# q of the first two units in packets of two positions, decay factors on GpSimd's queue, fillers behind the first scores

## The chip, the cores and the metric

The kernel runs on one core of a Trainium2 chip. The metric is the device time of one execution in microseconds. Profiles are of one execution; times inside them count from the start of its span.

## The reference

A retention block is followed by a multiplicative feed-forward block, both in float32 or wider:

```python
# q, k, v: (8 batches, 8 heads, 576 positions, 64)
scores = q @ k.T / sqrt(64)
Dmat   = where(i >= j, gamma[h] ** (i - j), 0)      # gamma[h] = 1 - 2**(-5-h)
ret    = (scores * Dmat) @ v
x      = ret.transpose(0, 2, 1, 3).reshape(4608, 512)
out    = ((x @ w1) * (x @ w2)) @ w3 @ w_out         # w1, w2: 512x1024, w3: 1024x1024, w_out: 1024x512
```

The four weights come in as 64-bit floats and are converted on the chip.

## The kernel before

The retention is computed in 20 units. A unit is a pair of batches and a chunk of positions; the chunks of a pair have 64, 128, 128, 128 and 128 positions. Units 0 to 4 are the first pair. Units are numbered g, with chunk c = g % 5.

The decay matrix is split into a factor for q, gamma^i / 8, and one for k, gamma^-j. They come as two small inputs, decay_q (8 heads x 576) and decay_k (576 x 8 heads). decay_q is fetched into dq as it lies, turned by five small TensorE transposes into the PSUM tile gps (L122) and copied by VectorE to gq (L125), where positions lie on partitions. decay_k is fetched straight into gk, by two transfers on ScalarE's DMA queue (L115, L116).

For each unit `load` (L87) fetches k, q and v: positions on partitions, and 2 batches x 8 heads x 64 values in each. A run that is contiguous in memory is one position of one head, 64 values, 256 bytes. Then

- `scale` (L195) multiplies q by gq (VectorE at L204 for units 0 and 1, ScalarE later) and v by gk (GpSimd at L204 for units 0 and 1);
- `front` (L207) transposes k and q by TensorE, two heads at a time, into a PSUM tile tp, and ScalarE copies it to kT and qT (L221), which have a head's values on partitions and positions along the row;
- `score` (L224) multiplies kT by qT into four PSUM tiles sc (L233); VectorE multiplies them by the causal mask into pm (L236);
- `state` (L240) adds k^T v to a state st (L255), which ScalarE copies to sb (L259);
- `pv_state` and `pv` multiply the state and pm into the output tiles xps (L274, L299), and ScalarE evicts them to xT (L306), the tokens of the second block.

The feed-forward block runs on blocks of tokens of 192 positions with one or two levels of Strassen's scheme; its VectorE sums (L149, L496, L533) and products (`up`, L528) begin at about 28 us and take the rest of the time. The weights are fetched in blocks by `load_block` on SP's queue (L342, L345), and converted by ScalarE (L395 to L397) and VectorE (L399, L402, L413, L426). `convert(n)` does n steps of that conversion.

All order is written out by hand: every engine takes its instructions in the order of the program text. The text at the start issues, on SP's queue, k and q of unit 0, weight block 0, v of unit 0, block 1, k and q of unit 1, block 2, v of unit 1, block 3, and then the loads of units 2, 3 and 4 with further blocks. ScalarE's queue issues dq and the two parts of gk. GpSimd makes the identity and the mask. TensorE runs ten products of the identity with itself (`idle`), and `keep_busy(n)` (L127) puts n more of them at other places; they write a PSUM tile that nobody reads. A float32 product shows as two passes in the profile.

The lines of the start that the change touches (L733 to L755):

```python
    scale(0, "q", engine=nc.vector)
    front(0, "k")
    keep_busy(4)
    front(0, "q")
    convert(2)
    score(0)
    scale(0, "v")
    state(0)
    convert_up_to(1)
    pv(0)()
    ...
    front(1, "k")
    keep_busy(4)
    scale(1, "q", engine=nc.vector)
    front(1, "q")
```

SBUF tiles come from pools, in which a tag has a fixed number of buffers that are taken in turn: "ld_q" has two, "T" five, "ab" two, "c" one. The PSUM pool "acc" has seven.

Of the kernel before, what the change touches and what calls it, by code (L numbers as in the profile page):

```python
# [8 lines left out]
F32 = mybir.dt.float32  # L9
# [4 lines left out]
ALU = mybir.AluOpType  # L14
# [5 lines left out]
def kernel(  # L20
# [13 lines left out]
    nc = tc.nc  # L34
    moe_w1, moe_w2, moe_w3, moe_w_out = (
        w.bitcast(I32).rearrange("r (c t) -> r c t", t=2) for w in (moe_w1, moe_w2, moe_w3, moe_w_out))
    B, H, S, D = q.shape
# [3 lines left out]
    P = 128  # L41
# [6 lines left out]
    NC = (S + P - 1) // P  # L48
    short = S - (NC - 1) * P
    sizes = [short] + [P] * (NC - 1)  # L50
    starts = [0] + [short + c * P for c in range(NC - 1)]
    G = NB2 * NC
    NB = 3
    TB = S // NB
    NT = 2 * TB // P
    KD = DM // P
    KF = DF // P
# [4 lines left out]
    const = ctx.enter_context(tc.tile_pool(name="const", bufs=1))  # L62
    wp = ctx.enter_context(tc.tile_pool(name="wp", bufs=1))
    ffn = ctx.enter_context(tc.tile_pool(name="ffn", bufs=2))
# [6 lines left out]
    pools = {}  # L71
# [9 lines left out]
    acc = acc_part.enter_context(tc.tile_pool(name="acc", bufs=7, space=PSUM))  # L81
# [3 lines left out]
    live = {}  # L85

    def load(g, names, engine=nc.sync):  # L87
        i, c = divmod(g, NC)
        sz = sizes[c]
        src = {"k": k, "q": q, "v": v}  # L90
        for nm in names:
            t = pools["ld"].tile([P, 2 * H, D], F32, tag="ld_" + nm, name="ld_" + nm)
            engine.dma_start(
                t[:sz], src[nm][2 * i:2 * i + 2, :, starts[c]:starts[c] + sz, :].rearrange("b h p d -> p (b h) d"))
            live[nm, g] = t

    dq = ffn.tile([P, 4, 2, TB], F32, tag="c", name="dq", bufs=1).rearrange("p a b s -> p (a b s)")[:H, :S]
    nc.scalar.dma_start(dq, decay_q)
    load(0, "k")
    load(0, "q")  # L100

    ident = const.tile([P, P], F32, tag="ident", name="ident")
    make_identity(nc, ident)
# [8 lines left out]
    gk = const.tile([P, NC, H], F32, tag="gk", name="gk")  # L112
    gq = const.tile([P, NC, H], F32, tag="gq", name="gq")
    gqs = const.tile([P, NP, S // 32], F32, tag="gqs", name="gqs")
    nc.scalar.dma_start(gk[:short, 0, :], decay_k[:short, :])  # L115
    nc.scalar.dma_start(gk[:, 1:, :], decay_k[short:, :].rearrange("(c p) h -> p c h", p=P))  # L116
    warm = acc.tile([P, P], F32, tag="acc", name="idle")
    for _ in range(10):
        nc.tensor.matmul(warm, ident, ident, start=True, stop=True)
    gps = acc.tile([P, NC, H], F32, tag="acc", name="gps")  # L120
    for c in range(NC):
        nc.tensor.transpose(gps[:sizes[c], c, :], dq[:, starts[c]:starts[c] + sizes[c]], ident[:H, :H])  # L122
    for c in (0, slice(1, NC)):
        n = short if c == 0 else P
        nc.vector.tensor_copy(gq[:n, c, :], gps[:n, c, :])  # L125

    def keep_busy(n):  # L127

        t = acc.tile([P, P], F32, tag="acc", name="idle")
        for _ in range(n):  # L130
            nc.tensor.matmul(t, ident, ident, start=True, stop=True)
# [63 lines left out]
    def scale(g, nm, scalar=False, engine=nc.gpsimd):  # L195
        c = g % NC
        sz = sizes[c]
        t, gam = live[nm, g], {"q": gq, "v": gk}[nm]
        t = t[:sz].rearrange("p (b h) d -> p b h d", b=2)
        if scalar:  # L200
            for h in range(H) if scalar is True else scalar:
                nc.scalar.mul(t[:, :, h, :], t[:, :, h, :], gam[:sz, c, h:h + 1])
            return
        engine.tensor_tensor(  # L204
            out=t, in0=t, in1=gam[:sz, c].unsqueeze(1).unsqueeze(3).to_broadcast([sz, 2, H, D]), op=ALU.mult)

    def front(g, names="kq"):  # L207
        c = g % NC
        sz = sizes[c]
        for nm in names:  # L210
            src = live[nm, g]
            dst = pools["fr"].tile([P, 2, NP, P], F32, tag=nm + "T", name=nm + "T",
                                   bufs=1 if nm == "k" and g >= NC else 2)
            for b in range(2):
                tp = acc.tile([P, NP, P], F32, tag="acc", name="tp")
                for p in range(NP):
                    h = b * H + 2 * p
                    nc.tensor.transpose(tp[:, p, :sz],  # L218
                                        src[:sz, h:h + 2, :].rearrange("p a d -> p (a d)"),
                                        ident[:sz, :sz])  # L220
                nc.scalar.copy(dst[:, b, :, :sz], tp[:, :, :sz])  # L221
            live[nm + "T", g] = dst

    def score(g):  # L224
        c = g % NC
        sz = sizes[c]
        kT, qT = live["kT", g], live["qT", g]
        pm = pools["fr"].tile([P, 2, 2, NP, P], F32, tag="pm", name="pm", bufs=1)
        for b in range(2):
            sc = [acc.tile([P, NP, P], F32, tag="acc", name="sc") for j in range(2)]  # L230
            for p in range(NP):
                for j, hs in enumerate(heads):
                    nc.tensor.matmul(sc[j][:sz, p, :sz], kT[hs, b, p, :sz], qT[hs, b, p, :sz],  # L233
                                     start=True, stop=True)
            for j in range(2):
                nc.vector.tensor_mul(pm[:sz, b, j, :, :sz], sc[j][:sz, :, :sz],  # L236
                                     mask[:sz, :sz].unsqueeze(1).to_broadcast([sz, NP, sz]))
        live["pm", g] = pm

    def state(g):  # L240
        c = g % NC
        sz = sizes[c]
        if c == NC - 1:
            return
        vs = live["v", g]
        kn = live["k", g]
        if c == 0:
            live["st"] = st_ps.tile([P, 2, NP, D], F32, tag="st", name="st")
        st = live["st"]

        for b in range(2):
            for p in range(NP):
                for j, hs in enumerate(heads):
                    h = b * H + 2 * p + j
                    nc.tensor.matmul(st[hs, b, p, :], kn[:sz, h, :], vs[:sz, h, :],  # L255
                                     start=(c == 0 and b == 0 and p == 0), stop=(c == NC - 2),
                                     skip_group_check=True)
        sb = pools["fr"].tile([P, 2, NP, D], F32, tag="sb", name="sb")
        nc.scalar.copy(sb, st)  # L259
        live["sb", g + 1] = sb  # L260
# [64 lines left out]
    def load_block():  # L325
        n = loaded[0]
        if n == len(blocks):
            return
        key, w = blocks[n]
        t = raw.tile([P, CV, 2], I32, tag="raw", name="raw", bufs=5)  # L330
        if key[0] in ("A", "w12"):
            if key[0] == "A":
                _, r, f = key
                t4 = t.rearrange("p (j c n) t -> p j c n t", j=2, c=2)
                parts = [(t4[:, j], w[:, f * P:(f + 1) * P]) for j, w in enumerate((moe_w1, moe_w2))]
            else:
                _, fp, _, r = key
                parts = [(t.rearrange("p (c n) t -> p c n t", c=2), w[:, fp * QC:(fp + 1) * QC])]
            for t2, src in parts:
                src = src[2 * r * P:2 * (r + 1) * P]  # L340
                if r == 0:
                    nc.sync.dma_start(t2, src.rearrange("(c p) n t -> p c n t", p=P))  # L342
                else:
                    for half in range(2):
                        nc.sync.dma_start(t2[heads[half]],  # L345
                                          src.rearrange("(c a d) n t -> a d c n t", a=2, d=D)[1 - half])
        elif key[0] == "wo":
            src = w.rearrange("(a i x) n t -> i a x n t", i=KF, x=BL)[key[1]]
            for a in range(QP):
                nc.sync.dma_start(t[a * BL:(a + 1) * BL], src[a])  # L350
        else:
            _, ft, h = key
            src = w[ft * P:(ft + 1) * P].rearrange("(j r) (a h f) t -> h a r j f t", r=BL, a=QP, h=DF // CV)
            for a in range(QP):
                nc.sync.dma_start(t[a * BL:(a + 1) * BL].rearrange("p (j f) t -> p j f t", j=P // BL), src[h, a])
        live["raw", n] = t
        loaded[0] += 1
# [105 lines left out]
    def convert(n):  # L463

        for _ in range(n):
            if go_on() is not None:
                return
# [105 lines left out]
    g = 0  # L573
# [152 lines left out]
    load_block()  # L726
    load(0, "v")
    load_block()
    load(1, "kq")
    load_block()  # L730
    load(1, "v")
    load_block()
# [1 line left out]
    front(0, "k")  # L734
    keep_busy(4)
    front(0, "q")
    convert(2)
    score(0)
    scale(0, "v")
    state(0)  # L740
    convert_up_to(1)
# [403 lines left out]
    g = NC  # L1145
# [9 lines left out]
    for g in first_pair:  # L1155
        n = (1, 1, 2, 2)[g - NC]
# [38 lines left out]
    g = 2 * NC - 1  # L1195
# [10 lines left out]
    g = 2 * NC  # L1206
# [14 lines left out]
    for g in range(2 * NC, G):  # L1221
        n = dealt[g - 2 * NC]
# [42 lines left out]
    g = G  # L1265
# [44 lines left out]
```

## Time and profile before

| | us |
|---|---|
| three runs | 835.0, 838.52, 838.6 |
| median of the three | 838.52 |
| the profiled execution | 836.28 |
| its span | 834.6 |
| TensorE busy in the span | 816.1 (98%) |
| VectorE busy | 545.4 (65%) |
| ScalarE busy | 291.7 (35%) |
| GpSimd busy | 216.2 (26%) |

The span runs from the first instruction to the last; what the profiled execution took beyond it, 1.7 us, lies around it. Busy shares are means over stages that have different limits. The page cuts the span in 40 slices of 20.9 us and gives a digit of tenths for each engine. A busy TensorE need not be at its peak, since the ends of matmuls are modelled.

### The profile page before, as it was taken

The numbers are of one execution on the slowest core, as the hardware profiler recorded it, in microseconds if no ns is written. First come the engines' busy times: TensorE is split into PE (matmuls) and PEld (weight loads), VectorE is DVE, ScalarE is ACT, GpSimd is POOL, SyncE is SP. The second block draws the span as 40 slices with busy tenths as digits, with TensorE's granted clock in tenths as the row PEclk, the third lists the DMA queues.
The fourth block names the chain that finished last, engine by engine and source line by source line (L and its number), as shares of the span: only waits on it lengthen the run. The fifth ranks groups of instructions, "written<-read, shape, count | busy, mean of one in ns | idle before, by whom it ended". The sixth has DMA issues, their size and how long they took to land.

```text
span 834.6 us, 15774 instructions
## 1 busy us (share of the span) xinstructions
PE 816.1 (98%) x6095; PEld 735.5 (88%) x6095; DVE 545.4 (65%) x962; ACT 291.7 (35%) x609; POOL 216.2 (26%) x247
## 2 busy tenths in 40 slices
PE   7999999999999999989999999999999999999998
PEld 7889999744888998779999889998889998899987
DVE  4899999992554558754657755577745667646653
ACT  4787556581111011245453024342034331033300
POOL 1000000001102353005556105555006461045600
PEclk8999999999999999999999999999999999999999
DMA  9995464446035668997876537978245453046311
GB/s 195 222 220 138 78 142 132 114 119 109 6 76 120 101 162 285 278 291 193 211 226 178 109 80 206 223 238 221 57 96 177 159 195 114 34 149 215 139 30 47
DMA packets 197484, 126.96 MB, mean 152 GB/s; under 512 B 157848, under 2 KB 179096, under 8 KB 197408
## 3 DMA queue, kind: packets, MB, share of 16 engines
q1 hardware_dynamic: 168560, 50.40, 29.5%
q0 software_dynamic: 11824, 63.31, 23.0%
q10 hardware_dynamic: 17024, 12.23, 5.3%
q8 instruction: 48, 0.79, 0.4%
q14 instruction: 28, 0.23, 0.1%
HBM read 103.62 MB, written 22.28 MB: 151 GB/s over the span
## 4 chain that ended last, share of the span: by engine, by line
PE 83%; DVE 7%; DMA 6%; issue 2%; SPq 1%; ACT 0%; POOL 0%; ACTq 0%; DVEq 0%
PE po L645 21%; PE up L1052 17%; PE up L528 14%; PE seed L1052 13%; PE ps L477 7%; PE xps L299 3%; PE sc L233 3%; PE xps L274 1%; DMA ld_v<-in_v_dram 1%; SPq L171 1%; PE tp L218 1%; DMA out_dram<-ot 1%; DMA ld_q<-in_q_dram 1%; PE st L255 1%; DVE ab L1024 1%
## 5 line engine op out<-in xcount | busy, mean ns | idle before, releaser
L645 PE MATMUL po<-w3o,ab 128*128 128x256 f32 x552 | 125.1, 381 | 4.0 <-DVE ot L649 3.2
L645 PEld LDWEIGHTS po<-w3o,ab 128*128 128x128 f32 x552 | 103.7, 190 | 20.8 <-DVE ot L649 5.1
L1057 POOL TENSOR_TENSOR cc<-cc 128x384 f32<-128x384 f32 x112 | 109.3, 1002 | 3.8 <-ACT cc L1075 2.4
L1064 DVE TENSOR_TENSOR cc<-seed,cc 128x384 f32<-128x384 f32 x88 | 48.6, 552 | 69.1 <-PE seed L1052 60.1
L181 POOL TENSOR_TENSOR bl_q<-bl_q,gqs 128x512 f32<-128x512 f32 (+1 forms) x26 | 25.9, 1014 | 187.8 <-DMA bl_q<-in_q_dram 184.4
L1052 PE MATMUL up<-xT,ra 128*128 128x192 f32 x384 | 73.5, 328 | 0.0
L528 PE MATMUL up<-xT,wA 128*128 128x192 f32 x384 | 70.7, 328 | 0.8 <-DVE xT L496 0.8
L533 DVE TENSOR_TENSOR c<-up,c 128x384 f32<-128x384 f32 x80 | 44.0, 550 | 39.6 <-PE up L528 39.2
L236 DVE TENSOR_TENSOR pm<-sc,mask 128x512 f32<-128x512 f32 (+1 forms) x80 | 45.3, 627 | 34.9 <-PE sc L233 34.8
L1064 DVE TENSOR_TENSOR cc<-up,cc 128x384 f32<-128x384 f32 x88 | 48.4, 550 | 29.8 <-PE up L1052 21.8
L528 PEld LDWEIGHTS up<-xT,wA 128*128 128x128 f32 x384 | 63.3, 190 | 2.2 <-PE up L528 1.1
L645 PE MATMUL po<-wB,forms 128*128 128x256 f32 x288 | 65.1, 379 | 0.0
L1052 PEld LDWEIGHTS up<-xT,ra 128*128 128x128 f32 x384 | 63.8, 190 | 1.0
L645 PEld LDWEIGHTS po<-wB,forms 128*128 128x128 f32 x288 | 54.7, 190 | 7.4
L1071 ACT COPY seed<-up 128x384 f32<-128x384 f32 x56 | 25.9, 463 | 100.2 <-PE up L1052 55.2
L953 POOL DMA_DIRECT2D ra<-kept x53 | 30.0, 565 | 117.7 <-PE seed L1052 88.5
L477 PE MATMUL ps<-wo,w3T 128*128 128x512 f32 x128 | 55.1, 592 | 0.0
L1052 PE MATMUL up<-ra 128*128 128x192 f32 x288 | 54.7, 326 | 0.0
L1052 PE MATMUL seed<-e,ra 128*128 128x192 f32 x256 | 50.9, 329 | 0.0
L477 PEld LDWEIGHTS ps<-wo,w3T 128*128 128x128 f32 x128 | 24.3, 190 | 30.1 <-issue 29.7
L1052 PEld LDWEIGHTS up<-ra 128*128 128x128 f32 x288 | 48.1, 190 | 0.1
L528 PE MATMUL up<-T,wS 128*128 128x192 f32 x256 | 46.7, 326 | 1.4 <-DVE wS L149 1.4
(129 smaller groups left out, 1467.5 us busy)
## 6 DMA issues: line engine op xcount, KB each, us to landing
ra<-kept POOLq DMA_DIRECT2D x53, 896.0 KB, 5.0
raw<-in_moe_w_dram SPq DMA_DIRECT2D x72, 128.0 KB, 3.0
out_dram<-ot ACTq DMA_DIRECT2D x50, 128.0 KB, 2.3
bl_q<-in_q_dram SPq DMA_DIRECT2D x192, 32.0 KB, 3.1
bl_k<-in_k_dram SPq DMA_DIRECT2D x136, 32.0 KB, 3.3
raw<-in_moe_w_dram SPq DMA_DIRECT2D x16, 256.0 KB, 6.4
ld_k<-in_k_dram SPq DMA_DIRECT2D x8, 512.0 KB, 6.2
raw<-in_moe_w_out_dram SPq DMA_DIRECT2D x32, 128.0 KB, 2.7
```

The source lines that it names most:

```text
L181: nc.gpsimd.tensor_tensor(out=part, in0=part, in1=gqs[:, :, n0:n0 + n].unsqueeze(3).to_broadcast([P, NP, n, BL]), op=ALU.mult)
L233: nc.tensor.matmul(sc[j][:sz, p, :sz], kT[hs, b, p, :sz], qT[hs, b, p, :sz], start=True, stop=True)
L236: nc.vector.tensor_mul(pm[:sz, b, j, :, :sz], sc[j][:sz, :, :sz], mask[:sz, :sz].unsqueeze(1).to_broadcast([sz, NP, sz]))
L477: nc.tensor.matmul(ps, live["w3T", ft][:, g, :], live["wo"][:, g, :], start=(g == 0), stop=(g == KF - 1))
L528: nc.tensor.matmul(ps[:, w, :], a[:, w, r, :], b[:, r, :], start=(new and w == r == 0), stop=(w == r == 1), skip_group_check=True)
L533: nc.vector.tensor_add(c[:, to], ps, c[:, sb])
L645: nc.tensor.matmul(ps[nm], a[A][:, f, :], live["W"][B][:, f, :], start=(f == 0 and not on), stop=(f == NP - 1), skip_group_check=True)
L953: engine.dma_start(ring[n % 3], kept[n % 14 // 7][nm])
L1052: nc.tensor.matmul(ps[:, w, :], weight_of(slot, a, w), B[b], start=(new and w == 0), stop=True, skip_group_check=True)
L1057: nc.gpsimd.tensor_tensor(out=o, in0=o, in1=i, op=ALU.add)
L1064: nc.vector.tensor_add(c[:, j], ps, with_add[:, j])
L1071: nc.scalar.copy(p6, p1)
```

## The change

- **q of units 0 and 1** is fetched by a new `load_pairs`. A partition now holds two neighbouring positions of one batch; the two batches lie on two halves of the partitions, and each is a transfer of its own. A contiguous run is two positions of a head, 512 bytes.
- **Their scaling** (`scale` for q of g < 2) is two instructions instead of one, one for each position of the pair (j), each for eight heads. They write a new tile q2, which takes one buffer of the tag "ab". The factors come from a new tile gq2, in which partitions run over batch and pair: decay_q is fetched twice over (once for each batch) into dq2[0] and dq2[1], transposed with a step of two positions (`decay_pairs`, two transposes), and copied by ScalarE.
- **Their transposes** are as many as before. ScalarE's copy puts the two positions back in order: it writes every second element of a row of qT.
- **Queues**: ScalarE's queue issues only dq2[0]. GpSimd's queue issues dq2[1], the two parts of gk and dq, after it has made the mask.
- **Order**: the ten idle products are followed by `decay_pairs(0)` only. The five transposes of dq and VectorE's two copies (now `decays`) come behind `score(0)`, after three more idle products and `decay_pairs(1)`.

```diff
+    def load_pairs(g):
+        i, c = divmod(g, NC)
+        n = sizes[c] // 2
+        t = live["q", g] = pools["ld"].tile([P, 2 * H, D], F32, tag="ld_q", name="ld_q")
+        for b in range(2):
+            nc.sync.dma_start(
+                t[b * n:(b + 1) * n].rearrange("p (h j) d -> p h (j d)", j=2),
+                q[2 * i + b, :, starts[c]:starts[c] + 2 * n, :].rearrange("h (i j) d -> i h (j d)", j=2))
+
...
-    nc.scalar.dma_start(dq, decay_q)
+    dq2 = [ffn.tile([H, 2, sizes[c]], F32, tag="T", name="dq2", bufs=5) for c in range(2)]
+    def by_batch(c):
+        return decay_q[:, starts[c]:starts[c] + sizes[c]].unsqueeze(1).to_broadcast([H, 2, sizes[c]])
+    nc.scalar.dma_start(dq2[0], by_batch(0))
     load(0, "k")
-    load(0, "q")
+    load_pairs(0)
...
-    nc.scalar.dma_start(gk[:short, 0, :], decay_k[:short, :])
-    nc.scalar.dma_start(gk[:, 1:, :], decay_k[short:, :].rearrange("(c p) h -> p c h", p=P))
+    nc.gpsimd.dma_start(dq2[1], by_batch(1))
+    nc.gpsimd.dma_start(gk[:short, 0, :], decay_k[:short, :])
+    nc.gpsimd.dma_start(gk[:, 1:, :], decay_k[short:, :].rearrange("(c p) h -> p c h", p=P))
+    nc.gpsimd.dma_start(dq, decay_q)
...
-    gps = acc.tile([P, NC, H], F32, tag="acc", name="gps")
...
+    def decays():
+        gps = acc.tile([P, NC, H], F32, tag="acc", name="gps")
...
+    def decay_pairs(c):
+        gp2 = acc.tile([P, 2, H], F32, tag="acc", name="gp2")
+        n = sizes[c]
+        for j in range(2):
+            nc.tensor.transpose(gp2[:n, j, :], dq2[c].rearrange("h b (i j) -> h j (b i)", j=2)[:, j], ident[:H, :H])
+        nc.scalar.copy(gq2[:n, c], gp2[:n])
+
+    decay_pairs(0)
...
+        if nm == "q" and g < 2:
+            if not g:
+                live["q2"] = ffn.tile([P, 2 * KF, TB], F32, tag="ab", name="q2").rearrange("p f t -> p (f t)")
+            n = 2 * H * D
+            to = live["q", g] = live["q2"][:, g * n:(g + 1) * n].rearrange("p (h d) -> p h d", d=D)
+            for j in range(2):
+                engine.tensor_tensor(out=to[:sz, j * H:(j + 1) * H],
+                                     in0=t[:sz].rearrange("p (h j) d -> p j h d", j=2)[:, j],
+                                     in1=gq2[:sz, c, j].unsqueeze(2).to_broadcast([sz, H, D]), op=ALU.mult)
+            return
...
-                nc.scalar.copy(dst[:, b, :, :sz], tp[:, :, :sz])
+                if nm == "q" and g < 2:
+                    nc.scalar.copy(
+                        dst[:, :, :, :sz].rearrange("p b m (i j) -> p m b i j", j=2)[:, :, :, :, b],
+                        tp[:, :, :sz].rearrange("p m (b i) -> p m b i", b=2))
+                else:
+                    nc.scalar.copy(dst[:, b, :, :sz], tp[:, :, :sz])
...
-    load(1, "kq")
+    load(1, "k")
+    load_pairs(1)
...
     score(0)
+    keep_busy(3)
+    decay_pairs(1)
+    decays()
     scale(0, "v")
```

More of the change, by code (lines that the diff above doesn't have):

```diff
@@ L119 @@
         nc.tensor.matmul(warm, ident, ident, start=True, stop=True)
-    gps = acc.tile([P, NC, H], F32, tag="acc", name="gps")
[L121 to L125, printed above, removed]
+    def decays():
+        gps = acc.tile([P, NC, H], F32, tag="acc", name="gps")
+        for c in range(NC):
+            nc.tensor.transpose(gps[:sizes[c], c, :], dq[:, starts[c]:starts[c] + sizes[c]], ident[:H, :H])
+        for c in (0, slice(1, NC)):
+            n = short if c == 0 else P
+            nc.vector.tensor_copy(gq[:n, c, :], gps[:n, c, :])
+    gq2 = const.tile([P, 2, 2, H], F32, tag="gq2", name="gq2")
+    def decay_pairs(c):
[5 more added lines that the diff above has]
+    decay_pairs(0)
     def keep_busy(n):
```

## The prediction

> **What bounds the kernel now.** I read the page's totals and slices first, then the chain of waits of the first 60 us, then one-microsecond stages of that stretch, and last the transfers in it. From the page:
>
> ```profile
> PE   7999999999999999989999999999999999999998
> ...
> DVE  4899999992554558754657755577745667646653
> ...
> DMA  9995464446035668997876537978245453046311
> ```
>
> TensorE is busy nearly everywhere except in the first of 40 slices (20.9 us each), where it has 7 tenths. There, and in the next two, the DMA engines are at 9 tenths. VectorE is at 4 tenths in the first slice and at 8 or 9 in the next six. The change lies in the first 20 us, so its worth is what it takes from that ramp; afterwards the sequence of work is the old one, begun earlier or later. The chain of waits there:
>
> ```profile
> 8.98 9.33 DMA ld_q<-in_q_dram
> 18.31 0.02 issue
> 18.33 1.24 DVE ld_q L204
> 19.57 0.09 issue
> 19.66 1.94 PE tp L218 x8
> 21.60 2.06 PE sc L233 x16
> 23.66 2.46 DVE pm L236 x4
> ```
>
> The columns are start, length, what. Unit 1's q, issued at 8.98, lands at 18.31; then come its scaling, its transposes and its scores, and the mask product on VectorE can start only at 23.66. From there VectorE is nearly full: 9.69 us of 10 in the stage 40 to 50, 9.35 in 50 to 60. So the ramp is one transfer, then one TensorE chain, then VectorE. The stages show at which clock that chain runs (columns: stage, its length, busy PE, PEld, DVE, ACT, POOL, granted clock, DMA share, GB/s):
>
> ```profile
> 10.00:11.00 1.00, 0.42 (x16) 0.29 (x10) 0.94 (x3) 0.94 (x3) 0.71 (x1) 1.00 1.13 243
> 11.00:12.00 1.00, 0.00 (x0) 0.00 (x0) 0.47 (x2) 0.69 (x1) 1.00 (x1) 1.00 1.27 207
> ...
> 13.00:14.00 1.00, 1.00 (x35) 1.00 (x33) 0.96 (x3) 0.57 (x2) 0.00 (x0) 0.78 1.35 217
> 14.00:15.00 1.00, 0.85 (x16) 0.66 (x14) 0.96 (x2) 0.97 (x3) 0.00 (x0) 0.50 1.34 218
> ...
> 23.00:24.00 1.00, 1.00 (x14) 1.00 (x14) 0.36 (x1) 0.97 (x2) 1.00 (x1) 0.60 1.00 234
> 24.00:25.00 1.00, 1.00 (x28) 0.88 (x30) 1.00 (x3) 0.55 (x2) 0.65 (x1) 1.00 1.27 260
> ```
>
> TensorE has nothing from 10.4 to 12.2, and some 3 us after that hole begins the clock is halved, for about 10 us. The transfers have two packet sizes; two stretches of the DMA view, 12.7 to 14.9 us and 16.5 to 17.6 us, separate them:
>
> ```profile
> DMA packets 1888, 0.48 MB, mean 218 GB/s; under 512 B 1888, under 2 KB 1888, under 8 KB 1888
> ...
> DMA packets 404, 0.36 MB, mean 329 GB/s; under 512 B 61, under 2 KB 404, under 8 KB 404
> ```
>
> The first is all 256-byte packets (k, q and v): 16 x 2.2 us / 1888 = 18.6 ns of one engine each. The second is mostly 1 KB weight packets: 44 ns on average, about 48 without the 61 small ones.
>
> [...]
>
> **The change, part by part.**
>
> 1. Packets. q of units 0 and 1 goes from 1024 and 2048 packets of 256 B to half as many of 512 B. A straight line through 18.6 ns at 256 B and 48 ns at 1 KB gives 28.4 ns at 512 B, so a pair saves 37.2 - 28.4 = 8.8 ns. There are 1536 pairs, 96 per engine: 0.85 us. q of unit 1 took longer than that mean: k before it landed at 8.34 + 6.6 = 14.9, q 3.4 us later, 26 ns for each of an engine's 128 packets. At that price of the slowest engine a pair saves some 16 ns, 1.6 us in all. I take 1.2 us for the landing of q of unit 1 and of what follows; low end 0.3 (engines bound by bytes), high end 1.8.
> 2. SP's queue. Each q becomes two issues, one more of about 0.65 us (the row at 1.60). Behind them are the weight blocks and v. SP runs ahead: k of unit 1 is issued at 8.34, while the block before it is needed and lands at 12.6. That 4 us backlog hides 0.65 us; without it the cost would be 0.65 per unit.
> 3. Decays. ACT's queue loses three of four issues (0.60, 0.56, 0.61 us); its table load can begin near 1.5 instead of 2.69. Nothing waited for that. The 576 packets of gk leave the stretch before q of unit 0 lands: from 5 to 6 us they hold the ACT queue's 30.4% of the engines. q of unit 0 then lands some 0.5 us before its 6.8. GpSimd gets four issues behind its mask (end 1.62). The nearest rows are 0.56 us (an output block) and 1.2 us (a v load), so the last leaves at 3.9 to 6.4; landings from that queue took 5.0 to 6.8 us under load, hence 8 to 13 for the last one, dq, and earlier for gk. GpSimd itself next works at 10.29.
> 4. Unit 0's front. Before, five transposes and two DVE copies (0.26 us) precede the scaling at 6.87. After, two transposes and one ACT copy (about 0.2): scaling near 6.65. Scaling becomes two half instructions of about 0.68 (the row of 128x512 at L149) in place of 1.22: +0.14, but the first half can be transposed meanwhile. The interleaved ACT writes have no row; the nearest, L395 reading two bytes of every eight, costs 0.78 against 0.72. I take +0.06, ends 0 and +0.6. All this lies in VectorE's waits for weights (1.18 us before 12.65): nothing on the path.
> 5. Fillers. Three idle products are six passes of 0.145 us (L131, 1.16 for eight) = 0.87 us; seven small transposes are about 0.9 more (gps: five in 0.64). They run from about 10.2 to 12.0, in the hole that ends at 12.24 when v is scaled. They cost nothing there; without the hole, 1.8 us. The clock should then stay full. At full clock unit 1's eight transposes take 1.04 instead of 1.94 (row at 36.33), the first half of the scores about 1.05 instead of 2.1.
>
> **Sum.** q of unit 1 lands at 17.1. Half scaling 0.68, then the second half, its transposes (0.52), the last ACT copy (0.59) and half the scores: the mask product at about 17.1 + 1.36 + 0.52 + 0.6 + 1.05 = 20.6, not 23.66: 3.0 us earlier. But not all of that survives. The loads of units 2 to 4 only gain the 1.2 us, and they are next in line: v of unit 3 lands at 38.33 + 9.3 = 47.6 and VectorE takes it at 48.21, a slack of 0.6; q of unit 4 is already waited for (0.36 us at 57.18), with 0.5 us of slack on VectorE behind it. So the shift that goes through is 1.2 + 0.5 = **1.7 us**. After 70 us the DMA share falls to 0.26 and TensorE carries the shift to the end. The profiled execution took 836.28 (span 834.6 and 1.7 around it): it would be 834.6. The runs are 835.0, 838.52 and 838.6; with the profiled one the mean is 837.1, which I use as the level since the median stands 2.2 above the profiled execution. Forecast: **835.4**.
>
> **Rivals.**
>
> - *The whole TensorE gain counts.* In 20 to 22 us the DMA engines are only at 0.56: SP sat in one issue of 4.08 us and nothing new was asked for. If fewer packets close that gap too (about 1.5 us), the loads no longer cap the shift and 3.0 + 1.5 = 4.5 us arrive: 832.6. Against it: the engines are at 1.27 again from 24 us, so the gap was short and the queue behind it long.
> - *The clock falls anyway*, because [...]q's wait near 17 us makes a new hole. Then only the packets count: -1.2, 835.9. This also covers the change not doing what it says.
> - *GpSimd's queue delivers late (slower).* PE takes the decay transposes in order, ahead of state, pv and the transposes of k of unit 1. Between 12.24 and the transposes of q of unit 1 it has 1.15 + 1.63 + 1.04 + 1.16 = 5.0 us of work at full clock, and q is ready at 17.8. So dq must land by about 12.8; each microsecond later is a microsecond lost. At 19 us the loss is 6.2, less the 1.7 gained: +4.5, 841.6. For it: the first software transfer is untried this early (the first stands at 304 us), and SP's backlog is in front of the engines. Against it: its issues at 304 us took 3.20 for four, as later ones did, and the loads are 2 to 18 KB.
>
> **How the numbers follow.** About 0.5% (4.2 us) is what a measurement of this kernel can tell from no change. The forecast has 0.52, the clock rival 0.16, the whole gain 0.20, the late queue 0.12. The first two stay within 0.5%, so faster 0.20, same 0.68, slower 0.12. The forecast's own effect runs from -0.3 to -3.1 around a level uncertain by 1.8; with most of the whole-gain case the range is 832.0 to 839.0, leaving out the late queue.
>
> **What would show it.** Right: q of unit 1 landing near 17, granted clock 1.00 throughout 13 to 24, the mask product of unit 1 near 20.6, then a new VectorE wait for v of unit 3 near 45. Wrong: PE waiting on gps for DMA, or q landing after 18.

## The result and the profile after

| | before | after |
|---|---|---|
| runs (us) | 6: 835.0 to 838.6, median 836.67 | 6: 842.99 to 846.33, median 845.73 |
| profiled execution, span | 836.28, 834.6 | 843.01, 841.3 |

The ratio is **1.0097, 95% interval 1.0077 to 1.0118**: the change costs about 1%. The forecast was 835.4, from 832 to 839. It was wrong in sign and in size. The two profiled executions differ by 6.7 us, the medians by 9.1: the one profiled after is among the two fastest of its six, so some 2 us of the loss stand in no trace.

The slices of the page after, in the order of those of before (TensorE, VectorE, DMA):

```profile
PE   6999999999999998999999999999999999999998
...
DVE  3899999992553556854566764677755557545653
...
DMA  9995364446035669996876536979255363145411
```

The first slice has lost a tenth of TensorE and of VectorE, and so has the 16th (315 to 336 us): TensorE 8 for 9, VectorE 6 for 8. So at least two places count, and the change touches only the first. To find what each is worth I matched VectorE's instructions of the two traces by tile and position and took the difference of their starts: +2.2 us at 30 us and unchanged to 310; **+7.2** at 314; +5.6 at 325; +3.7 at 360; +6.8 from 374 to the end. Three steps: +2.2, about +5 with some of it given back, +3.1. (The fall between 350 and 360 is before's own: its TensorE waits 2.1 us there, and in every other trace but one the shift falls by 1.5 to 2.4 us.)

**The first step.** The chain of waits of the first 30 us after (start, length, what):

```profile
8.70 4.95 SPq L103
13.65 0.04 issue
13.69 7.12 DMA ld_q<-in_q_dram
...
20.91 0.70 DVE q L235
21.61 0.14 issue
21.75 0.64 PE tp L258 x4
22.39 0.02 issue
22.41 1.23 ACT qT L262 x2
23.64 0.04 issue
23.69 3.35 PE sc L278 x32
27.04 1.27 DVE pm L281 x2
```

It is the chain of before, but SP's queue now stands in it. Unit 1's q was one issue at 8.98; now the first half holds SP until 13.65 and the second half is only asked for at 13.69, lands at 20.8, and the scores run mostly at half clock (granted 0.63, 0.50 and 0.50 in the stages from 24 to 27; 3.35 us for 32, where 32 took 2.06 in e1_act). SP's queue of before, then after:

```profile
8.98 3.05 SPq L93 DMA_DIRECT2D ld_q<-in_q_dram  x1
12.08 2.92 SPq L342 DMA_DIRECT2D raw<-in_moe_w_dram  x2
```

```profile
8.70 5.62 SPq L103 DMA_DIRECT2D ld_q<-in_q_dram  x2
14.37 2.18 SPq L387 DMA_DIRECT2D raw<-in_moe_w_dram  x2
```

The weight block behind q is issued 2.3 us later too, but it is not what sets the shift. The last part of unit 1's mask product starts at 27.62 in place of 25.45, 2.2 us later, and the shift at 40 us follows this start within 0.6 us in every trace. In e14_after_clock (below) the block is issued 1.5 us later than before, and the shift is -0.7. The transfers from 13.6 to 20.9 us, before and then after (the DMA view's total line):

```profile
DMA packets 4802, 1.69 MB, mean 232 GB/s; under 512 B 4194, under 2 KB 4801, under 8 KB 4801
```

```profile
DMA packets 3530, 1.55 MB, mean 212 GB/s; under 512 B 2006, under 2 KB 3529, under 8 KB 3529
```

There are a quarter fewer packets, and no more bytes per microsecond. In part little was asked for: from 14 to 15 us, behind SP's long issue, the engines moved 131 GB/s (a stage below). From 15 to 20 us it was still 229 GB/s against 254. The landings show the rest of the delay. A transfer has 16 reports in the trace, which I take as one for each engine, and VectorE starts on q of unit 1 only behind the last: at 18.33 before, with the last report at 18.31 and the median at 16.78. After, half of the engines have delivered the second half of q at 17.84, the last one at 20.81, and its scaling starts at 20.91. From 7 us on the last engine is 1.3 to 3.0 us behind the median (I call this the lag); before, mostly 0.3 to 0.5 until 15 us and then 1.5.

The clock (stages as in the prediction; the number behind the busy times of the five engines is the granted clock):

```profile
13.00:14.00 1.00, 0.03 (x2) 0.03 (x2) 0.17 (x2) 0.00 (x0) 0.91 (x1) 1.00 1.16 178
14.00:15.00 1.00, 1.00 (x34) 1.00 (x36) 0.52 (x2) 0.00 (x0) 0.00 (x0) 1.00 0.62 131
...
20.00:21.00 1.00, 0.00 (x0) 0.00 (x0) 0.09 (x1) 0.00 (x0) 0.00 (x0) 1.00 1.29 232
...
24.00:25.00 1.00, 1.00 (x16) 1.00 (x14) 0.00 (x0) 0.97 (x2) 0.01 (x1) 0.63 0.65 187
```

In this execution the clock stayed full through 13 to 24. TensorE stood idle for q from 19 to 21.7, and a drop came at 24.3.

**The second step** is 290 us after the last line that the change touches. VectorE's waits between 300 and 330 us, after:

```profile
DVE kT L220 <- DMA bl_k<-in_k_dram: 8.2, 1, 8.2
```

and of before:

```profile
DVE kT L190 <- DMA bl_k<-in_k_dram: 3.2, 1, 3.2
```

kT of unit 9 is transposed by VectorE from bl_k, which SP fetches in 16 transfers of 32 KB in packets of 128 B. At 304 to 306 us GpSimd starts to store the weight forms (kept, line L894 before). The DMA view by queue, 312 to 322 us, before and then after (q0 is GpSimd's queue, q1 is SP's):

```profile
q0 software_dynamic: 938, 3.23, 90.3%
q1 hardware_dynamic: 1439, 0.31, 14.9%
```

```profile
q0 software_dynamic: 849, 3.00, 94.0%
q1 hardware_dynamic: 1168, 0.17, 10.0%
```

The packets of the two queues are of one order in number, but a stored packet has 3.5 KB on average (3.00 MB / 849) and a loaded one 128 or 256 B, and the stores' packets have nine tenths of the engines' time (94.0%, the loads' 10.0%). For each packet loaded, some 2.6 KB were stored (3.00 MB / 1168). How an engine shares its time between the queues is not shown.

**The third step**, 366 to 374 us, goes with a clock at half (granted 0.50) from 372.4 to 375.8; TensorE pauses before it for the scaling of unit 10's q. Before's profiled execution has no drop there.

### The profile page after: what moved, and what is told of

It reads as the page before. It is cut to its first block, busy times and chain, and to the rows that moved or that the text cites. A ratio compares the mean times of both kernels' runs of the same rounds, so it can differ in the third digit from the quotient of the medians.

```text
span 841.3 us, 15808 instructions
## 1 busy us (share of the span) xinstructions
PE 817.8 (97%) x6105; PEld 735.5 (87%) x6105; DVE 544.9 (65%) x964; ACT 292.4 (35%) x611; POOL 218.8 (26%) x251
## 4 chain that ended last, share of the span: by engine, by line
PE 84%; DVE 6%; DMA 4%; SPq 2%; issue 2%; ACT 1%; POOL 0%; ACTq 0%; DVEq 0%
PE po L690 22%; PE up L1101 17%; PE up L573 15%; PE seed L1101 13%; PE ps L522 7%; PE sc L278 3%; PE xps L344 3%; PE xps L319 1%; DMA bl_k<-in_k_dram 1%; PE st L300 1%; DMA kept<-wA 1%; PE tp L258 1%; SPq L201 1%; DMA ld_q<-in_q_dram 1%; DVE ab L1073 1%
## 5 line engine op out<-in xcount | busy, mean ns | idle before, releaser
L690 PEld LDWEIGHTS po<-w3o,ab 128*128 128x128 f32 x552 | 103.7, 190 | 18.7 <-DVE ot L694 3.1
L522 PEld LDWEIGHTS ps<-wo,w3T 128*128 128x128 f32 x128 | 24.3, 190 | 30.1 <-issue 29.7
```

What stands on the lines that cost most here:

```text
L522: nc.tensor.matmul(ps, live["w3T", ft][:, g, :], live["wo"][:, g, :], start=(g == 0), stop=(g == KF - 1))
L690: nc.tensor.matmul(ps[nm], a[A][:, f, :], live["W"][B][:, f, :], start=(f == 0 and not on), stop=(f == NP - 1), skip_group_check=True)
```

## The experiments

All ratios are to the kernel before, run on the same chip (medians of before 836.67, 836.81, 836.92, 838.25 and 835.98 in the five comparisons). Each result gives the median in us, then the ratio with its 95% interval. Shifts are against before's profile. "kT waits" means VectorE's wait for bl_k near 314 us. There is one profile per kernel.

### Which part: queues, packets, fillers

**e1_act**: the changed kernel, all decay transfers on ScalarE's queue.

```diff
-    nc.gpsimd.dma_start(dq2[1], by_batch(1))
-    nc.gpsimd.dma_start(gk[:short, 0, :], decay_k[:short, :])
...
-    nc.gpsimd.dma_start(dq, decay_q)
+    nc.scalar.dma_start(dq2[1], by_batch(1))
+    nc.scalar.dma_start(gk[:short, 0, :], decay_k[:short, :])
...
+    nc.scalar.dma_start(dq, decay_q)
```

> The changed kernel with its four later decay transfers back on ScalarE's queue; pairs and fillers stay. Theory A (small transfers through GpSimd's queue put one or two DMA engines about 2 us behind from 6 us on, and every load waits for its last engine): the last engine of q of unit 0 is no longer 1.6 us behind the middle one, q of unit 1 lands near 17 to 18 instead of 20.8, unit 1's mask product starts near 21 to 22 instead of 25.3, and the time is at or below the kernel before (0.996 to 1.000). Theory B (the pair packets or the two half transfers themselves are slow): q of unit 1 still lands near 20 to 21 and the ratio is near 1.01.

841.28, 1.0048 (1.0028 to 1.0068). The early step is gone (shift -0.3 from 30 us on), and the last engine is 0.2 to 0.4 behind the median until 12.6 us. But theory A also wanted q of unit 1 before 18 and no loss of time, and neither came. SP's queue:

```profile
10.21 2.74 SPq L103 DMA_DIRECT2D ld_q<-in_q_dram  x2
12.99 2.22 SPq L387 DMA_DIRECT2D raw<-in_moe_w_dram  x2
```

The second half is out by 12.95, not 14.3; q lands at 18.6, still not earlier than before's 18.3. An earlier q would hardly have helped here, as the chain shows:

```profile
9.57 6.43 DMA ld_k<-in_k_dram
...
18.07 1.71 PE idle L161 x8
19.78 1.72 PE tp L258 x8
```

It runs through unit 1's k, which lands at 16.0, and through four of the old idle products, which stand in TensorE's order ahead of q's transposes and here run at about half clock (eight passes take 1.92 us; 1.91 in before at a granted 0.50, 1.06 in after at 1.00). The step at 314 is all there (+4.9).

**e8_gk_only**: the changed kernel with only gk on GpSimd's queue.

```diff
-    nc.gpsimd.dma_start(dq2[1], by_batch(1))
-    nc.gpsimd.dma_start(dq, decay_q)
+    nc.scalar.dma_start(dq2[1], by_batch(1))
+    nc.scalar.dma_start(dq, decay_q)
```

> The changed kernel with only the two gk transfers left on GpSimd's queue; dq2 of the second unit and dq go by ScalarE's. Theory A1 (any small software transfer beside the pair loads makes one or two DMA engines lag): last engine 1 us or more behind the median from 6 us on, q of unit 0 scaled at 7.6 or later, mask product of unit 1 near 25, time as the changed kernel, 844 to 846. Theory A2 (it is the dq and dq2 transfers, whose rows are long, or the number of software transfers): lags of 0.2 to 0.5, q of unit 0 near 6.7, mask product of unit 1 near 23.4, time as with all decays on ScalarE's queue, 840 to 842.

843.98, 1.0091 (1.0070 to 1.0112). The lags are 0.5 to 1.5, the mask product of unit 1 starts at 24.0 and the shift is +0.9, which lies between the two theories. kT waits 8.5.

**e2_gk_soft**: the kernel before with gk (two transfers) on GpSimd's queue.

```diff
-    nc.scalar.dma_start(gk[:short, 0, :], decay_k[:short, :])
+    nc.gpsimd.dma_start(gk[:short, 0, :], decay_k[:short, :])
...
```

> The kernel before with only the two gk transfers moved to GpSimd's queue; no pairs, no fillers, dq stays on ScalarE's. Theory A: the lag appears near 6 us as in the changed kernel, unit 1's q lands 1.5 to 2.5 us later than 18.3, and the ratio is 1.002 to 1.010. Theory B: nothing changes, 0.999 to 1.001, q of unit 1 near 18.3.

839.01, 1.0025 (1.0015 to 1.0034). There is no early lag, and the shift is -0.4: the kernel is a little slower, as theory A said, but not for its reason; what costs the 0.25% is open. **e12_soft_no_pairs** adds dq and one dq2 there, into tiles that nothing reads:

```diff
...
+    nc.gpsimd.dma_start(dq2, decay_q[:, starts[1]:starts[1] + sizes[1]].unsqueeze(1).to_broadcast([H, 2, sizes[1]]))
-    nc.scalar.dma_start(gk[:short, 0, :], decay_k[:short, :])
+    nc.gpsimd.dma_start(gk[:short, 0, :], decay_k[:short, :])
...
+    nc.gpsimd.dma_start(dq3, decay_q)
```

> The kernel before, q loads unchanged in 256 B packets, with the four transfers of the changed kernel on GpSimd's queue (gk in two, and dq and one dq2, these two into tiles that nothing reads). Theory A3 (the software transfers make one or two DMA engines late, whatever the packets of the loads): last engine 1.3 us or more behind the median from 6 us on, q of unit 0 scaled at 7.6 or later, mask product of unit 1 near 25, time 839 to 841. Theory A4 (only together with the pair loads): lags of 0.3 to 0.5, mask product of unit 1 at 23 to 24, time 836.5 to 839.

838.54, 1.0000 (0.9987 to 1.0013), with lags of 0.1 to 0.3 up to q of unit 1. So four small transfers on GpSimd's queue cost nothing measurable beside loads of whole units. With the pair loads, q of unit 0 lags by 0.8 to 1.6 us when some of them are there (after, e5, e8, e14) and by 0.2 to 0.3 when all are on ScalarE's queue (e1, e11, e15). That speaks for the two together, but loads in halves alone lag as well (next run), so the cause of the lag is not settled.

**e9_halves**: the kernel before, q of units 0 and 1 in two transfers of half the partitions, packets still 256 B.

```diff
...
+                for b in range(2):
+                    engine.dma_start(
+                        t[b * n:(b + 1) * n],
+                        q[2 * i:2 * i + 2, :, starts[c] + b * n:starts[c] + (b + 1) * n, :].rearrange(
+                            "b h p d -> p (b h) d"))
...
```

> The kernel before with q of units 0 and 1 loaded in two transfers of half the partitions each, still in 256 B packets; nothing else is changed. Theory D (what the pairs bring by being two transfers: two more of SyncE's outstanding loads and half the DMA work each, whatever the packet): q of unit 1 scaled near 18.5 in place of 18.3, as with the pairs and all decays on ScalarE, so that the packets of 512 B bring nothing; if also the block loads of 299 to 310 come late against the stores, kT waits 7 to 8 us and the time is 839 to 842. Rival (two half transfers cost time and the packets win it back): q of unit 1 scaled at 19.3 or later; time up to 838.

839.02, 1.0024 (1.0008 to 1.0039). The profile is of the slowest of its 22 runs, 848.04 us (kT waits 10.7 in it), so it may not be typical. In it q of unit 1 is scaled at 20.4. With one transfer that was 17.9 to 18.9 (before, e2, e3, e4, e6, e7, e10, e12, e13), with pairs and the decays on ScalarE's queue 18.7 to 19.5 (e1, e11, e15). The first half holds SP for 3.96 us, and from 7 us on the lags are 0.8 to 2.1, with nothing on GpSimd's queue. The median engine varies less: it delivers q of unit 1 at 18.5 here, at 17.3 to 17.4 in e1, e11 and e15, and at 16.4 to 17.2 with one transfer. By this measure the second transfer costs about 1.5 us and the packets win about 1.1 back. That favours the rival, as far as one trace of the halves can tell.

**e3_fillers**: the kernel before with six fillers behind the first scores.

```diff
     score(0)
+    keep_busy(6)
     scale(0, "v")
```

> The kernel before with six idle products behind the first scores (twelve passes of 0.145 us, as long as the changed kernel's three fillers and seven small transposes), nothing else. If the clock fell because of the hole at 10.4 to 12.2, it stays at 1.00 through 13 to 24; the mask product of unit 1 then starts 1 to 2 us before 23.64, and the loads hold the gain to 0.5 us or so: ratio 0.998 to 1.000. If the clock matters fully, 0.996. If the fillers delay the state, 1.001.

838.11, 1.0010 (1.0000 to 1.0021). The clock stays full until 20.2, then drops. The mask product starts at 23.4, not 1 to 2 us earlier as expected: it waits for q, and the drop falls on its scores (3.17 us for 32). In this trace the fillers do what they should and bring nothing.

### The step at 314 us

**e4_delay**: the kernel before with eight fillers on TensorE near 105 us.

```diff
     up(0, 0, 2, conv=[2, 1, 1, 2, 2], tail=False)
     owed.append(1)
+    keep_busy(8)
     att_part.close()
```

> The kernel before with eight idle products (about 2.2 us of TensorE) put at about 105 us, where TensorE is full and the loads of the first units are over. It asks whether a plain shift of 2.2 us is what makes the changed kernel lose a further 4.5 us at 310 to 376 us (kT of unit 6 lands 10.3 us after its last issue instead of 5.3). If the shift alone does it: TensorE waits about 3 us for kT near 320 and the total is +5 to +7 us, ratio 1.006 to 1.008. If not: +2.2 us, ratio 1.0026, and the wait is not there.

840.16, 1.0038 (1.0026 to 1.0049). The shift is +1.6 from 110 us on, but kT waits only 2.2, and the shift is still +1.6 at 325. A late program alone does not make the step.

**e7_tags**: the kernel before with one dummy tile of tag ab and two of tag T, so that buffers rotate as in the changed kernel.

```diff
+    for _ in range(2):
+        nc.gpsimd.memset(ffn.tile([P, 2, TB], F32, tag="T", name="dq2", bufs=5)[:1, 0, :1], 0.0)
+    nc.gpsimd.memset(ffn.tile([P, 2 * KF, TB], F32, tag="ab", name="q2")[:1, 0, :1], 0.0)
```

> The kernel before with three tiles allocated and touched by a tiny GpSimd memset, in the places that q2 and dq2 take in the changed kernel (one buffer of tag ab, two of tag T), so that the rotation of these buffers is that of the changed kernel; nothing else is changed. Rival (the rotation makes token sums or products of the feed-forward part wait for another buffer, and so sets the 5 us at 314): kT waits 7 to 8 us and the time is 839 to 841. Theory C (an offset of loads against stores): same time within 0.2%, 835.5 to 838.

836.02, 0.9997 (0.9981 to 1.0012); kT waits 0.2. So it is not the rotation of the buffers.

**e5_after_hold** and **e6_before_hold**: the changed kernel and the kernel before, with twelve tiny memsets on GpSimd ahead of its first stores.

```diff
+        def late():
+            if h == 0:
+                for _ in range(12):
+                    nc.gpsimd.memset(hold, 0.0)
+            send([(0, 0, None), (4 * P, 1, None)])
+
-        return [tt(...), lambda: send([(0, 0, None), (4 * P, 1, None)])]
+        return [tt(...), late]
```

> The changed kernel with twelve tiny memsets on GpSimd (128x64) ahead of its first kept stores near 306 us, so that SyncE's last bl_k and ld_k packets meet them later. Theory C (the 5 us at 314 are a collision of SyncE's last block loads with GpSimd's kept stores, decided by an offset of about 1 us): the wait of kT for bl_k falls from 8.2 to under 3 us, the shift against the kernel before stays near +2 through 314 to 360, and the time falls by 2 to 5 us to 841 to 844. Rival (what makes kT wait is the loads' own start or their buffers): the wait stays near 8 us and the time near 846.

> The kernel before with the same twelve memsets ahead of the kept stores. Theory C: its wait of kT for bl_k falls from 3.2 to about 1 us or less, and the time is 0 to 2 us less than before (835 to 837). If holding the stores costs by itself (they are read back later), the time is 1 to 3 us more, and the run of the changed kernel with the memsets is read against this one: theory C expects their difference to be 3 to 5 us in place of 9.

e5: 839.32, 1.0020 (1.0007 to 1.0033), where the changed kernel had 1.0097: some 6 us were regained by 2.4 us of memsets ahead of GpSimd's stores, more than expected. Its wait for bl_k:

```profile
DVE kT L221 <- DMA bl_k<-in_k_dram: 0.3, 1, 0.3
```

and what the queues moved in it from 306 to 312 us (SP's loads have the engines nearly to themselves):

```profile
q1 hardware_dynamic: 3044, 0.37, 39.6%
q0 software_dynamic: 28, 0.11, 6.4%
```

e6: 836.29, 1.0001 (0.9984 to 1.0018). Its kT waits 0.7 in place of 3.2, and the time is the same: before has no such loss to regain. Against before's profile it is 3.1 us ahead at 314 and 0.8 at 325, as much as it was ahead of the wait, so before's wait of 3 us costs nothing that lasts.

**e10_sp_late** is the mirror: the kernel before, three small loads more in SP's queue ahead of bl_k.

```diff
+        if g == 2 * NC - 1 and nm == "k":
+            for j in range(3):
+                nc.sync.dma_start(hold[:, j, :], k[j, 0, :P, :BL])
```

> The kernel before with three small loads more (128 packets of 128 B each, into a tile that nothing reads) in SyncE's queue ahead of the bl_k loads of unit 9 (near 299 us): some 1.5 us of issue. This is the mirror of holding the stores. Theory C (the offset of SyncE's last block loads against GpSimd's kept stores decides): ld_k is issued 6 us or more after the first store in place of 5.1, kT waits 7 to 9 us for bl_k in place of 3.2, and the time is 3 to 6 us more, 839.5 to 842.5. Rival (the pairs bring the wait by something else): kT waits 4 to 5 us and the time is 837 to 839.

852.96, 1.0168 (1.0155 to 1.0181): 14 us for 1.9 us of issue, about three times what I expected. The wait of kT is

```profile
DVE kT L194 <- DMA ld_v<-in_v_dram: 17.4, 1, 17.4
```

(the view names ld_v, but the last engine of bl_k lands at 328.4, 0.3 us before kT starts). Over all traces the wait follows one measure, the time from GpSimd's first kept store to SP's issue of ld_k, which is next in its queue behind bl_k:

| from first store to ld_k's issue (us) | kernels | kT waits (us) |
|---|---|---|
| 1.7 to 2.4 | e5, e6, e11, e15 | 0 to 0.7 |
| 3.7 to 5.4 | before, e2, e3, e4, e7, e12, e13 | 0.2 to 4.5 |
| 5.6 to 6.6 | after, e1, e8, e14 | 7.6 to 8.5 |
| 8.0 and 9.5 | e9, e10 | 10.7 and 17.4 |

The measure is partly an effect (in the chain after, SP's own issues grow from 0.45 to 1.2 us there), so the two mirrored experiments carry the cause, not the table.

### Both costs out, and the clock

**e11_act_hold**: the changed kernel with the edits of e1_act and e5_after_hold.

> The changed kernel with both costs taken away: all decay transfers on ScalarE's queue, and the twelve memsets ahead of the kept stores. If software transfers beside the pairs (2 to 3 us) and the collision at 314 (5 us) are the whole loss, the time is that of before, 836 to 838, and the pairs with the fillers are worth nothing within 0.2%. If something else of the change costs, it is 839 or more; if the pairs bring a gain that the two costs hide, it is under 835.5.

838.57, 1.0005 (0.9990 to 1.0020). Four versions of the changed kernel side by side:

| | stores as they were | stores held |
|---|---|---|
| decays on GpSimd's queue | 1.0097 | 1.0020 |
| decays on ScalarE's queue | 1.0048 | 1.0005 |

The collision, SP's last block loads meeting GpSimd's stores, is worth 0.77% or 0.43%, the queue 0.49% or 0.15%; they do not simply add, and the 0.15% is within the noise. Without both, pairs and fillers are worth nothing that can be measured here.

**e13_before_clock**, **e14_after_clock**, **e15_act_hold_clock**: before, after and e11_act_hold, with six fillers at TensorE's pause near 362 us.

```diff
-    front(g)
+    front(g, "k")
+    keep_busy(6)
+    front(g, "q")
```

> The kernel before with six filler products of 128x128 on TensorE ahead of the transposes of unit 10's q, near 362 us, where TensorE waits for ScalarE's scaling of q. Theory E (the shifts of +2.4 to +5.5 us between 360 and 374 in most profiles are the clock at half[...], let in by TensorE's pauses there): no drop of the clock between 360 and 376, and the time is near the fast end of the kernel before, 834.5 to 836.5, with a smaller spread. Rival (the fillers come too late or are too few): drop as without them, 837 to 838.5.

> The changed kernel with the same six fillers near 368 us. If the drop of the clock there (3.1 us of the 6.7 us between the two profiles) is a matter of the one profiled execution and not of the change, the time falls by as much as that of the kernel before does with them, by 0 to 2 us, and stays 7 to 10 us above it: 843 to 846. Rival (the change brings this drop and the fillers take it away): 840 to 842.5.

> The changed kernel with the decays on ScalarE's queue, the memsets ahead of the kept stores and the six fillers near 364 us: all three suspected costs out. Theory E: no drop of the clock there, 834 to 836.5, which would be the fastest of all here. If the pairs are worth nothing it equals the kernel before with the fillers within 0.15%; if they are worth their 0.85 to 1.6 us, it is 1 us or more under it.

836.41, 1.0004 (0.9992 to 1.0015); 844.69, 1.0118 (1.0088 to 1.0149); 839.24, 1.0051 (1.0035 to 1.0067). The drop is in none of the three profiles (before, e5, e8 and e11 lack it without fillers too). The stage where it was, in the changed kernel and then in e14:

```profile
370.00:375.00 5.00, 4.32 (x71) 3.45 (x69) 2.56 (x8) 1.78 (x5) 0.57 (x1) 0.74 0.89 262
```

```profile
370.00:375.00 5.00, 4.53 (x61) 3.60 (x57) 1.41 (x4) 2.20 (x7) 0.00 (x0) 1.00 0.92 274
```

The difference of after and before with the fillers in both stays 1% (844.69 to 836.41), so the third step is no cost of the change: the drop stands in the profiles of e2, e3, e4, e6, e7 and e12 too, kernels close to before. It seems to come and go between executions, and keeping it away brings the median nothing; in e13 the shift still grows by 1.4 us between 366 and 374, which may be what the fillers take. e14 shows one thing more: the early code of the changed kernel, unaltered, had a shift of -0.7 in that execution, and +2.2 and +3.1 in those of after and e5. e15 stands against e11 and against theory E: the same kernel with fillers that cost before nothing is 0.5% over before, and its profiled execution (836.9 us, among the fastest of its 16) doesn't show where the others lose it. That is open.

## Why the prediction was wrong, step by step

1. **Packets: failed, in the term for the landing.** q of unit 1 was to land 1.2 us earlier; it landed 2.5 us later (after 18, as the prediction named for a wrong one), and 0.3 later in e1_act. Two prices were off. A 512 B packet was put at 1.5 times a 256 B one by a straight line. In the records of single packets from 12 to 20.9 us a 256 B packet takes 24.3 ns on average in before, a 512 B one 38.9 after and 47 to 52 in e1, e5, e8, e11, e14 and e15: 1.6 to 2.1 times as much. And the 26 ns at "the slowest engine" was no price of a packet but a lag: in before the median engine delivers q 2.3 us after k (14.5 to 16.8), 18 ns for each of 128 packets, as elsewhere; only the last one needs 3.4 us. In e4, e6, e7 and e13 the last engine delivers the same q 0.8 to 1.6 us earlier than in before.
2. **SP's queue: failed.** "That 4 us backlog hides 0.65 us" was wrong twice. The issue of a half took 4.95 us of SP's time (2.06 in e1_act), not 0.65; what held it is not shown. The issue of the whole q at 8.98 before, 3.05 us, was the row to read. And what stood behind it was the other half of the same q, which has no backlog to hide in.
3. **Decays: failed where they were costed at nothing.** The gain was there: on ScalarE's queue q of unit 0 is scaled at 6.45 to 6.65, as forecast. With transfers on GpSimd's queue it was scaled at 7.2 to 8.0, and its last engine was 0.8 to 1.6 us late. By the medians that queue costs 0.5% (1.0097 against 1.0048); that the lag is the reason is argued, not shown. The case priced for that queue, dq landing late, didn't happen: it landed at 10.7, within the forecast, and TensorE never waited for it.
4. **Unit 0's front: right.** In e1_act the scaling starts at 6.59 (6.65 forecast), and the interleaved copies put nothing on the path.
5. **Fillers: partly right, worth nothing.** The clock stayed full through 13 to 24 in after and e14. In e1, e5, e8, e11 and e15, with the same pairs and fillers, it dropped at 15.3 to 17.5, where TensorE had waited 1.1 to 2.5 us for unit 1's k, which lands later with the pairs (15.8 to 16.9, before 14.9). The prediction counted the hole ahead of v and not the one ahead of k. That a hole brings the drop was inferred from before's profile alone (a wait of 1.8 us until 12.24, half clock from 13.6 for 10.2 us): in after the clock fell only at 24.3, behind a wait of 2.8 us until 21.75.

**The sum** failed last and most: that the shift of the ramp goes unchanged to the end, whatever its size. At 314 us kT waited 8.2 us in place of 3.2, and holding the stores back took 1.0097 to 1.0020. I looked for what might absorb a gain, not for what a shift in SP's stream might run into. At 311 to 314 us before had 3.2 us of kT's wait on record beside GpSimd's stores, and that line was the warning. The slower rival had the queue right and the mechanism wrong; its 841.6 was still short by 4 us.

**Open**: why the versions with pairs put SP's last loads 5.6 us or more behind the first store. It isn't the buffers (e7_tags), a late program (e4_delay) or the early lag (e14 has a shift of -0.7 and kT still waits 7.6). e9_halves shows it in one execution with two transfers alone. Nor do these versions start further apart: from SP's first bl_k to the first store it is 3.6 to 3.8 us in after, e1, e8 and e14, and 3.6 to 3.9 in e3, e4 and e13, where kT waits 2.2 to 4.5. So the collision is shown to be the loss, and how pairs in q's first loads lead to it 300 us later is not.

## What to carry to other kernels

Split a load across halves of the partitions only if what it brings is more than a second transfer costs (here about 1.5 us by the median engine of e9_halves, of which the packets won about 1.1 back), and price a load by its last engine as well as by the mean packet (3.4 and 2.3 us for q of unit 1 in before); don't take a lag for a price. Where a small-packet load shares the engines with large-packet stores of another queue, a microsecond or two of order can decide (2.4 us of memsets regained some 6 us in e5, 1.9 us of issue cost 14 in e10): see in the profile which is asked for first, and put the loads ahead. When a change shifts one queue against another, go through all later places where both are busy, not only those that the change touches.

## What was not expected of the hardware

- In three executions with the same early code (after, e5, e14) the last of 16 engines delivered q of unit 1 3.0, 2.8 and 1.2 us behind the median, with four small transfers on GpSimd's queue beside half-partition loads in 512 B packets. With such transfers beside whole loads in 256 B packets (e12) it was 0.1 us.
- In half-partition loads a 512 B packet took 39 to 52 ns in the records, 1.6 to 2.1 times as long as a 256 B packet in whole loads (24 ns), so little was left of the saving.
- 1.9 us more in SP's queue cost 14 us. From 308 to 328 us its packets of 128 and 256 B had 13.6% of the engines, and the stores' packets of 3.5 KB had 83.1%.
- The half clock moved between executions of the same early code: e14 had none at all there, after had 3.4 us of it from 24.3, and in e5 it began at 15.3.
